# Chunk 0's block inverses: halves joined by small matmuls beside the first hops, and keys 7 and 8 loaded from GpSimd's queue

## The chip, the cores and the metric

The kernel runs on one core of a Trainium2 chip. The metric is device time in microseconds from launch to end. The core has five engines, each of which works through its own list of instructions in order: TensorE (PE: matrix products, which end in the accumulator memory PSUM), VectorE (DVE: elementwise work and reductions), ScalarE (ACT: functions and scaled copies), GpSimd (POOL: masks and a few elementwise operations) and SyncE (SP, which here only issues transfers). A transfer (DMA) is issued from the queue of an engine, here SP's or POOL's, and waits in that queue for what stands ahead of it. Engines wait for each other through semaphores.

## The reference, cut to what matters

Two parts. First a delta-rule attention over 4 batches, 8 heads, 768 positions and a head size of 48; then a feed-forward layer on its output (3072 tokens, 384 to 2048 to 384).

```python
k_n = k / (norm(k) + 1e-06)
for t in range(S):
    y[:, :, t] = einsum('bhd,bhde->bhe', q[:, :, t], state)
    v_old = einsum('bhde,bhd->bhe', state, k_n[:, :, t])
    state = state + beta[t] * einsum('bhd,bhe->bhde', k_n[:, :, t], v[:, :, t] - v_old)
h = x @ w_in
out = (h * sigmoid(1.702 * h)) @ w_out
```

The loop over positions is computed in chunks of 128. Within a chunk the recurrence is a lower triangular system per batch and head, with the scaled products of keys below its diagonal. The kernel cuts it into four blocks of 32 positions, inverts each 32x32 block on the diagonal, and applies the blocks one after another.

## The kernel before, in words

A unit is one chunk of one batch (all 8 heads); there are 24, numbered chunk by chunk, so units 0 to 3 are chunk 0 of batches 0 to 3. Per unit the key tile `KN` is turned into `kT` (`turn`, line 398), multiplied with itself into `G` (`gram`, line 375), and the queries `QP` are turned into `QS` and multiplied with the keys into the score matrix `M` (`scores`, line 565), which GpSimd masks (`select`, line 604).

`invert` (line 441) inverts all 128 diagonal blocks of a chunk at once, one (batch, head, block) in each partition, on DVE. `NT` holds the blocks, `YB` the growing inverses, each as 32x32 numbers in a row. First come 15 steps, each a product and a reduction, that invert the upper left and lower right 16x16 halves together. Then come eight pairs of a product and a reduction (`dots`, line 453) that work out the off-diagonal half from the two inverted halves and the 16x16 block between them. For chunk 0 the result is transposed by 32x32 squares (`YT`), so that partitions are positions again, and multiplied by the scale in `zs` into one tile `XB` for each unit.

The sequence of the blocks is done in hops. `together` (line 796) does, for one or two units, `solve` (block inverse times values, into `psU`, copied by ACT into `US`) and `below` (products that carry a solved block to those below it, into `psR`, subtracted from `V` by DVE). `hops(a, b)` (line 952) interleaves two units over eight hops. In chunk 0 units 0 and 1 go first, then units 2 and 3. After each pair `put_out` (line 960) computes outputs (`psY`), state (`ST`) and the transfers of the result into `xT`.

Beside this stands the conversion of the feed-forward weights. The weights arrive as 64-bit floats and are rebuilt as 32-bit ones on DVE and ACT, a step at each `fill` (line 294). `fetch_in` (line 174) fetches a quarter of `w_in` in twelve transfers; the fourth quarter is fetched when the first is converted (line 284), into the same place. `fetch_out` (line 190) does the same for `w_out`. `hidden` (line 700) and `written` (line 724) are the feed-forward products; `hidden` yields so that the products can be woven in (`feed`, line 1007).

The order of everything up to chunk 1 is written out by hand in the last part (from line 885), and most operations there are pinned to program order on their engine. `keys()` (line 965) normalizes and turns the keys of units 4 to 8 in small steps; `ahead_of(preparing, 1)` takes one. `warm` (line 132) issues matmuls with no use of their result: 46 of them (`NY`) in the middle of `invert`, then 11 (`NU`) in a hop of the first path, 3 (`NA`) in the last two. From unit 3 on `woven` (line 840) does the rest of the chunks.

Tiles come from pools with a fixed number of buffers. `spare` (line 437) takes a buffer of the pool `gT` (8 buffers) for other use in the start. `KN` has seven buffers, so key 7 goes where key 0 was, and 8 where 1 was. In the kernel before, keys 7 and 8 are loaded from SP after both outputs of the first pair.

## Time and profile before

| | |
|---|---|
| time, median of 3 runs | 781.71 us (781.21 to 783.49) |
| profiled execution, its own time | 782.82 us |
| its span, first to last instruction | 780.8 us |
| granted TensorE clock, mean | 0.965 |
| PE busy | 753.3 us (96%), 8165 matmul instructions |
| DVE busy | 457.1 us (59%) |
| ACT busy | 243.1 us (31%) |
| POOL busy | 125.3 us (16%) |
| shares of the chain that ended last | PE 83%, DVE 11%, DMA 3%, ACT 2%, issue 1% |
| first solve of chunk 0 (`psU`) starts at | 44.73 us |
| first output product of unit 0 (`psY`) starts at | 60.16 us |
| first output product of unit 2 starts at | 98.67 us |
| first DVE operation of chunk 1's inversion starts at | 114.95 us |

The profile gives the start of each instruction from the start of the span. A matmul of 32-bit floats is two instructions in it. Busy shares of a whole span say little here, because the start (up to some 160 us) is limited by other things than the rest. The chain of work that ended last is followed back from the end, at each step to what released the instruction; a filler matmul that nobody waits for can stand in it when it is the instruction before on PE. Nearly all instructions stand on one line (102, a helper that pins them), so they are told apart by the tiles that they write and read.

### The profile page before, as it was taken

To read this page: it belongs to the slowest core of one execution; us is meant where nothing else is said; L and a number is where in the kernel's file an instruction comes from. 1 tells how busy PE (TensorE), PEld (TensorE's weight loads), DVE (VectorE), ACT (ScalarE), POOL (GpSimd) and SP (SyncE) were. 2 spreads that over 40 slices of the span, in tenths; PEclk is the share of its full clock that TensorE was granted. 3 is DMA by queue.
4 is the path that set the end of the run, shared out by engine and by line. 5 is a ranking of instruction groups with operands and counts; after the bars stand their busy time and mean duration, and the time that the engine had idled before them with its cause. 6 is when DMAs were issued, how large, how long until landed. Compare 5 with 4: busy or idle time off the path is not lost.

```text
span 780.8 us, 18832 instructions
## 1 busy us (share of the span) xinstructions
PE 753.3 (96%) x8165; PEld 564.1 (72%) x8165; DVE 457.1 (59%) x935; ACT 243.1 (31%) x536; POOL 125.3 (16%) x130
## 2 busy tenths in 40 slices
PE   7898799699999999999999999999999999999997
PEld 6677688365678678678678678678678678687684
DVE  5989679987977566666666666666665531000000
ACT  4563642234333223123123123123123123121110
POOL 6311310011221221221221221221210000000000
PEclk8599899879999999999999999999999999999999
DMA  9954940453332142142142142142130020000000
GB/s 158 177 68 92 220 90 1 120 159 89 75 96 62 37 98 51 36 97 55 32 98 54 33 98 54 33 97 55 33 76 12 22 44 1 15 13 1 26 1 21
DMA packets 132610, 50.73 MB, mean 65 GB/s; under 512 B 107456, under 2 KB 128064, under 8 KB 132528
## 3 DMA queue, kind: packets, MB, share of 16 engines
q1 hardware_dynamic: 130192, 41.47, 25.1%
q0 software_dynamic: 2336, 8.06, 4.2%
q8 instruction: 64, 1.05, 0.6%
q14 instruction: 18, 0.15, 0.1%
HBM read 32.08 MB, written 16.25 MB: 62 GB/s over the span
## 4 chain that ended last, share of the span: by engine, by line
PE 83%; DVE 11%; DMA 3%; ACT 2%; issue 1%; SPq 0%; POOL 0%; DVEq 0%; POOLq 0%; ACTq 0%
PE po L102 29%; PE ph L102 27%; PE psU L102 5%; PE psY L102 5%; PE psQ L102 4%; PE psG L102 4%; PE psT L102 3%; DVE P L102 3%; PE ps_warm L102 2%; PE psR L102 2%; DVE YB L102 2%; DVE tmp L102 2%; DVE w_out L102 1%; DVE NT L102 1%; DMA KN<-in_k_dram 1%
## 5 line engine op out<-in xcount | busy, mean ns | idle before, releaser
L102 PE MATMUL po<-w_out,gT 128*128 128x384 f32 x768 | 269.6, 500 | 7.2 <-ACT ksq L102 5.2
L102 PE MATMUL ph<-xT,w_in 128*128 128x256 f32 x1152 | 262.6, 384 | 0.3
L102 PEld LDWEIGHTS ph<-xT,w_in 128*128 128x128 f32 x1152 | 215.6, 191 | 32.9 <-issue 1.3
L102 PEld LDWEIGHTS po<-w_out,gT 128*128 128x128 f32 x768 | 143.2, 193 | 99.3 <-ACT ksq L102 5.6
L102 DVE TENSOR_TENSOR V<-V,psR 64x384 f32<-64x384 f32 (+1 forms) x96 | 53.3, 556 | 193.2 <-PE psR L102 190.3
L102 ACT ACTIVATE gT<-ph 128x512 f32<-128x512 f32 x96 | 56.5, 596 | 140.1 <-PE ph L102 140.0
L102 DVE TENSOR_TENSOR P<-NT,YB 64x8 f32<-64x8 f32 (+31 forms) x190 | 89.5, 471 | 5.4
L102 ACT COPY US<-psU 32x384 f32<-32x384 f32 x92 | 43.2, 470 | 135.6 <-PE psR L102 123.8
L102 DVE TENSOR_REDUCE YB<-P 64x4 f32<-64x8 f32 (+31 forms) x190 | 80.9, 426 | 6.5
L102 PEld LDWEIGHTS psU<-V,XB 32*32 32x32 f32 x1536 | 58.1, 106 | 33.6 <-issue 28.9
L102 PE MATMUL psU<-V,XB 32*32 32x48 f32 x1536 | 68.7, 204 | 0.6 <-issue 0.3
L605 POOL TENSOR_SCALAR_AFFINE_SELECT M<-M 128x1024 f32<-128x1024 f32 x20 | 26.4, 1321 | 249.8 <-DVE M L102 170.3
L102 PE MATMUL psR<-US,G 32*32 32x48 f32 x2208 | 60.6, 204 | 0.0
L102 PEld LDWEIGHTS psR<-US,G 32*32 32x32 f32 x2208 | 51.2, 106 | 1.6 <-ACT w_out L102 1.1
L102 PE MATMUL psQ<-QS,kT 48*128 48x176 f32 (+1 forms) x384 | 37.6, 341 | 2.7 <-ACT QS L102 2.7
L102 PE MATMUL psG<-kT 48*128 48x128 f32 x384 | 33.6, 315 | 3.8 <-ACT kT L102 2.6
L102 PEld LDWEIGHTS psQ<-QS,kT 48*128 48x128 f32 x384 | 31.1, 209 | 5.9 <-ACT QS L102 4.4
L102 DVE TENSOR_TENSOR P<-NT 64x256 f32<-64x256 f32 (+7 forms) x40 | 34.5, 862 | 0.4
L102 PEld LDWEIGHTS psG<-kT 48*128 48x128 f32 x384 | 28.6, 214 | 7.7 <-ACT kT L102 3.0
L102 DVE TENSOR_REDUCE NT<-P 64x64 f32<-64x1024 f32 (+7 forms) x40 | 32.6, 815 | 1.4
L102 ACT COPY o<-po 128x384 f32<-128x384 f32 x24 | 11.5, 479 | 61.7 <-issue 39.2
L102 ACT COPY M<-psQ 128x256 f32<-128x256 f32 x68 | 22.9, 377 | 22.2 <-DVE V L102 16.1
(98 smaller groups left out, 602.8 us busy)
## 6 DMA issues: line engine op xcount, KB each, us to landing
Nd<-G SPq DMA_DIRECT2D x16, 512.0 KB, 3.5
QP<-in_q_dram SPq DMA_DIRECT2D x24, 192.0 KB, 4.2
V<-in_v_dram SPq DMA_DIRECT2D x24, 192.0 KB, 3.4
out_dram<-o SPq DMA_DIRECT2D x24, 192.0 KB, 2.5
NT<-Nd SPq DMA_DIRECT2D x20, 128.0 KB, 2.6
Yd<-YS SPq DMA_DIRECT2D x20, 128.0 KB, 2.5
XB<-Yd SPq DMA_DIRECT2D x20, 128.0 KB, 3.0
KN<-in_k_dram POOLq DMA_DIRECT2D x13, 192.0 KB, 3.7
```

The costliest lines, as they stand in the source:

```text
L102: return lambda *a, **kw: tc.keep_in_program_order(op(*a, **kw))
L605: (pool if self.n < B else nc.gpsimd).affine_select(out=self.M, in_=self.M, compare_op=ALU.is_gt, fill=0.0, base=0, pattern=[[0, H], [1, 1 ...
```

## The change

For chunk 0, `invert` ends after the 15 steps on the halves. DVE then transposes the inverted halves twice: `YT` with positions of the block's rows in the partitions, and `Yb`, the same blocks the other way round. The off-diagonal half of each unit is made by the new function `joined`: for each head and block a 32x32 by 32x16 product on PE with the diagonal block in `D_`, an ACT copy back into `D_`, a second product with `Yb` (16 rows contracted), a subtraction on DVE into `YT`, and the product with the scale that gives `XB`. A unit's join is 64 matmuls, in two stages of 32.

The joins of unit 0 and the first stage of unit 1 stand ahead of the first hop; the others go into the hops of the first path. So do the scores of unit 1 and the first part of those of unit 2, and the scaling of the values of units 2 and 3; the rest of the scores of units 2 and 3 goes into the second path. Fillers in `invert` become 30, issued after the DVE steps in program order; in hops 0 to 5 of the first path they become 5.

The order of the first transfers changes: values 0 and 1 and query 0 go before the first quarter of `w_in`, GpSimd waits for value 1 (`landed`) before the second quarter, keys 4 to 6 go ahead of the third quarter. Keys 7 and 8 are loaded by GpSimd's queue, each after the output of the unit whose buffer it takes. `zs` moves from the pool slot `ksq` into the buffer that `late_U` uses, and the small ACT operation at the start uses the gelu function instead of a copy.

```diff
--- before.py
+++ after.py
@@ -55,7 +55,7 @@
     GB = 8
 
     XR = DP - D
-    NW, NA, NY, NU = 14, 3, 46, 11
+    NW, NA, NY, NU = 14, 3, 30, 11
     NQ = DFF // 4
     NPC = DFF // 8
     NS = C * C + C
@@ -137,7 +137,7 @@
             pe.matmul(ps, lhsT=ones[:, 0:128], rhs=ones, start=True, stop=True)
 
     table = cpool.tile([128, 1], F32, name="table")
-    act.activation(table, ident[:, 0:1], ACT.Copy)
+    act.activation(table, ident[:, 0:1], ACT.Gelu_apprx_sigmoid)
 
     w_out = cpool.tile([128, FC, DM], F32, name="w_out")
 
@@ -477,6 +477,11 @@
             red(diag(Yf, i, [[BS, i]]), P, axis=AX.X, op=ALU.add, negate=True)
             yield 0.0
 
+        if c == 0:
+            vec.transpose(YT.rearrange("p d i -> p i d"), Y.rearrange("p j i -> p i j"))
+            vec.transpose(Yb.rearrange("p d j -> p j d"), Y)
+            yield 0.0
+            return
 
         X1 = N[:, 0:HS, HS:]
         if c <= 1:
@@ -497,8 +502,6 @@
             yield 0.0
         for i in range(0, HS, Q):
             n = i + Q
-            if c == 0 and i == HS - 3 * Q:
-                warm(NY, vec.memset)
             dots(
                 Y[:, 0:HS, HS + i : HS + i + Q],
                 A[:, :, 0:n].rearrange("p j (o l) -> p j o l", o=1).broadcast_to([np, HS, Q, n]),
@@ -506,18 +509,6 @@
                 HS, Q, n, True,
             )
             yield 0.0
-        if c == 0:
-            T = wk.tile([128, BS, BS], F32, tag="P", name="YT")
-            vec.transpose(T.rearrange("p d i -> p i d"), Y.rearrange("p j i -> p i j"))
-            for b in range(B):
-                XB = wk.tile([128, H, BS], F32, tag="XB", name="XB", bufs=4)
-                tt(
-                    XB, T[:, b * H : (b + 1) * H],
-                    zs[:, 5, b].broadcast_to([128, H, BS]), op=ALU.mult,
-                )
-                inverse[b] = XB
-                yield 0.0
-            return
         YS = wk.tile([128, BS, BS], F32, tag="P", name="YS")[part]
         tt(YS, Y, bc, op=ALU.mult)
         dma = sync if c < 3 else nc.sync.dma_start
@@ -536,6 +527,35 @@
                 inverse[c * B + b] = XB
         yield 0.0
 
+
+    def joined(b):
+
+        HS = BS // 2
+        d = slice(b * H, (b + 1) * H)
+        blocks = [slice(blk * BS, (blk + 1) * BS) for blk in range(NB)]
+        ps = ps_moe.tile([128, H, HS], F32, tag="moe", name="psZ")
+        for h in range(H):
+            for r in blocks:
+                pe.matmul(
+                    ps[r, h, :], lhsT=D_[r, b, h, :], rhs=YT[r, b * H + h, HS:],
+                    start=True, stop=True,
+                )
+        Z = D_[:, b, :, 0:HS]
+        act.copy(Z, ps)
+        yield
+        ps = ps_moe.tile([128, H, HS], F32, tag="moe", name="psC")
+        for h in range(H):
+            for r in blocks:
+                u = slice(r.start, r.start + HS)
+                pe.matmul(
+                    ps[r, h, :], lhsT=Yb[u, b * H + h, :], rhs=Z[u, h, :],
+                    start=True, stop=True,
+                )
+        vec.tensor_tensor(YT[:, d, HS:], YT[:, d, HS:], ps, op=ALU.subtract)
+        XB = wk.tile([128, H, BS], F32, tag="XB", name="XB", bufs=4)
+        vec.tensor_tensor(XB, YT[:, d], zs[:, 5, b].broadcast_to([128, H, BS]), op=ALU.mult)
+        inverse[b] = XB
+        yield
 
     def bank(name, shape=(128, H, D)):
         return ps_seq.tile(list(shape), F32, tag="seq", name=name)
@@ -904,21 +924,31 @@
         pool.memset(KN[i][:, :, D:DP], 0.0)
     landed = cpool.tile([128, 1], F32, name="landed")
     pool.tensor_copy(landed, KN[B - 1][:, 0, 0:1])
+    def first_queries(b):
+        load(b, ((QP, q),), sync)
+
+    for b in range(HB):
+        load_values(b, sync)
+    first_queries(0)
     fetch_in(0, other_queue)
-    for b in range(B):
-        load(b, ((QP, q),), sync)
-    for b in range(B):
+    pool.tensor_copy(landed, loaded[HB - 1][:, 0, 0:1])
+    for b in range(1, B):
+        first_queries(b)
+    for b in range(HB, B):
         load_values(b, sync)
     fetch_in(1, other_queue)
-    D_ = spare("blocks").rearrange("p (b h k) -> p b h k", b=B, k=BS)
-    fetch_in(2, other_queue)
     for n in range(B, len(KN)):
         load(n, ((KN, k),), sync)
+    D_ = spare("blocks").rearrange("p (b h k) -> p b h k", b=B, k=BS)
+    YT = spare("YT").rearrange("p (d i) -> p d i", i=BS)
+    Yb = spare("Yb").rearrange("p (d i) -> p d i", i=BS)
+    fetch_in(2, other_queue)
     for blk in range(NB):
         sync(out=bI[blk::NB, 1:], in_=betas[:, 1:, blk, :])
-    late_U = spare("U")[:, 0 : H * D + XR]
+    room = spare("U")
+    late_U = room[:, 0 : H * D + XR]
     pool.memset(late_U[:, H * D :], 0.0)
-    zs = wk.tile([128, 6, B, H], F32, tag="ksq", name="zs", bufs=1)
+    zs = room[:, 512 : 512 + 6 * B * H].rearrange("p (s b h) -> p s b h", s=6, b=B)
     psD = [ps_seq.tile([128, B, NP, BS], F32, tag="seq", name="psD") for _ in range(2)]
     warm(NW)
     for b in range(B):
@@ -935,19 +965,26 @@
     vec.transpose(
         NT.rearrange("p i k -> p k i"), D_.rearrange("p b h k -> p k (b h)")
     )
-    for b in range(B):
+    def values_scaled(s, hs):
+        for h in hs:
+            act.mul(s.V[:, h, :], s.V[:, h, :], zs[:, 4, s.b, h : h + 1])
+
+    for b in range(HB):
         gram(b)
-    inverting = invert(0)
-    pair = [new_step(n) for n in range(B)]
-    for n in range(B):
-        for _ in pair[n].scored:
-            pass
-    run(inverting)
-    for s in pair:
-        for h in range(H):
-            act.mul(s.V[:, h, :], s.V[:, h, :], zs[:, 4, s.b, h : h + 1])
-    for s in pair:
-        s.select()
+    pair = [new_step(n) for n in range(HB)]
+    run(pair[0].scored)
+    pair[0].select()
+    for b in range(HB, B):
+        gram(b)
+    pair += [new_step(n) for n in range(HB, B)]
+    for s in pair[:HB]:
+        values_scaled(s, range(H))
+    run(invert(0))
+    warm(NY)
+    joins = [joined(b) for b in range(B)]
+    next(joins[0])
+    next(joins[1])
+    next(joins[0])
 
     def hops(a, b):
 
@@ -986,17 +1023,29 @@
 
     preparing = keys()
     path = hops(*pair[:2])
+    beside_hops = {
+        0: lambda: next(joins[1]),
+        1: lambda: next(pair[1].scored),
+        2: lambda: (run(pair[1].scored), pair[1].select()),
+        3: lambda: next(joins[2]),
+        4: lambda: next(joins[3]),
+        5: lambda: next(joins[2]),
+        6: lambda: next(joins[3]),
+        7: lambda: next(pair[2].scored),
+    }
     for i in range(2 * NB):
         together(*next(path))
+        beside_hops[i]()
         fill(1)
         if i > 1:
             ahead_of(preparing, 1)
-        warm(NU if i < 6 else NA)
-    for s in pair[:2]:
+        if 3 <= i < 7:
+            values_scaled(pair[2 + (i - 3) // 2], range((i - 3) % 2 * NP, (i - 3) % 2 * NP + NP))
+        warm(NU // 2 if i < 6 else NA)
+    for n, s in enumerate(pair[:2]):
         put_out(s)
+        load(len(KN) + n, ((KN, k),), other_queue)
         fill(2)
-    load(7, ((KN, k),), sync)
-    load(8, ((KN, k),), sync)
     for n in range(B, B + 2):
         load(n, ((QP, q),), sync)
     for n in range(B, B + 2):
@@ -1017,8 +1066,14 @@
     gTs = [], []
     ffn.append(hidden(xTs[0], gTs[0], slice(0, NTH), 1.3, True))
     path = hops(*pair[2:])
+    beside_hops = {
+        0: lambda: (run(pair[2].scored), pair[2].select()),
+        1: lambda: next(pair[3].scored),
+        2: lambda: (run(pair[3].scored), pair[3].select()),
+    }
     for i in range(2 * NB):
         together(*next(path))
+        beside_hops.pop(i, lambda: None)()
         fill(2 if i < 5 else 3)
         if i > 2:
             feed()
```

## The prediction

> **What bounds the kernel now.** I read the page's slices first: the first seven show PE below full, its granted clock falling to half, and DVE near full. Then the chain that ended last, DVE's timeline for the stretch the chain shows as filler matmuls, and the busy time by stretch.

> The page's slices (one digit is a tenth of busy share, 19.5 us a slice):

> ```profile
> PE   7898799699999999999999999999999999999997
> DVE  5989679987977566666666666666665531000000
> PEclk8599899879999999999999999999999999999999
> ```

> DVE's timeline (start, length, then the instruction): the second half of chunk 0's inversion.

> ```profile
> 27.67 0.77 DVE L102 COPY NT<-YB 128x256 f32<-128x256 f32 x1
> ...
> 40.92 1.22 DVE L102 TENSOR_REDUCE YB<-P 128x64 f32<-128x1024 f32 x1
> 42.17 1.99 DVE L102 STREAM_TRANSPOSE YT<-YB 128x1024 f32<-128x1024 f32 x1
> 44.20 1.43 DVE L102 TENSOR_TENSOR XB<-YT,zs 128x256 f32<-128x256 f32 x4
> ```

> The chain over the same time and a later one:

> ```profile
> 37.77 6.60 PE ps_warm L102 x46
> 44.38 0.35 issue
> 44.73 0.83 PE psU L102 x16
> 45.56 1.31 PE ps_warm L102 x11
> 47.68 1.31 PE ps_warm L102 x11
> ...
> 70.91 4.03 DMA w_out<-in_moe_w_in_dram
> 75.00 5.62 DMA KN<-in_k_dram
> 80.70 0.52 ACT ksq L102
> 81.25 0.61 ACT G L102
> 81.90 1.12 PE psT L102 x4
> ```

> The chain names fillers, but they end at 44.38 and wait for nobody; the first solve at 44.73 needs XB, which DVE begins only at 44.20. So DVE's inversion, 16.76 to 44.6, sets the start of the hops. The second block is a transfer: key loads stand on SP behind twelve fetches of w_in, and ACT, in order, waits for one (7.2 us in the waits).

> Busy time by stretch (DVE's is the third figure):

> ```profile
> 30.00:40.00 10.00, 8.63 (x53) 6.64 (x52) 9.76 (x15) 5.98 (x20) 4.03 (x3) 0.50 1.03 187
> 60.00:70.00 10.00, 8.66 (x189) 7.66 (x186) 9.74 (x18) 5.28 (x13) 1.64 (x1) 1.00 0.05 13
> 70.00:80.00 10.00, 7.94 (x153) 6.00 (x151) 7.72 (x13) 2.15 (x4) 1.64 (x1) 0.83 1.09 197
> 80.00:90.00 10.00, 8.10 (x107) 6.46 (x108) 3.93 (x9) 7.12 (x12) 6.41 (x8) 0.66 1.18 252
> ```

> After the clock column come DMA share and GB/s: DMA is idle at 60 to 70, saturated at 70 to 90 while ACT waits, PE runs at 0.66 and DVE at 39%. From psY of unit 2 (98.67) on, DVE works almost without a gap to 162 and PE without one to 139; a shift there goes to the end.

> [...] the 46 fillers took 6.6 us; at 0.226 us (14 cold ones took 3.17) and 0.119 us (11 warm ones took 1.31) some 10 were cold. Short waits (1.34 and 0.68 us from 67.7 on) were enough to halve it at 71.5. [...] psD agrees, 64 instructions in 0.82 us, but with four column groups and one row group. [...] a key load takes a median 3.7 us from GpSimd, 4.6 from SP.

> **The change, part by part.**

> *Before the first hop.* DVE stops after its triangular steps (27.63), transposes YT (1.99, to 29.7) and Yb (the same shape, to 31.7). 14.5 us of DVE products go away. PE keeps four grams but only unit 0's score ahead of the fillers: the second gram ends at 16.87 as now, the score takes 3.8 (the period of the four at 22.5 to 37.7), two grams 2.83 each, so fillers begin at 26.4 and 30 of them (10 cold, 20 warm) take 4.7: 31.2. ACT scales 16 value slices, not 32 (7.32/2 = 3.7), done by about 31. Then the join of unit 0: a stage of 32 matmuls is 64 instructions. By psD's rate 64 x 12.8 ns = 0.82 us. The first stage of unit 0 to 32.0, of unit 1 to 32.8 with unit 0's ACT copy beside it (128x128, as `last`, 0.27), the second stage of unit 0 to 33.7, DVE's subtraction 0.3 (nearest: ST 128x192, 0.36), the XB product 1.43/4 = 0.36, handovers 0.1 each: the first solve at about 34.8 instead of 44.73. **-9.9.** Bounds: 33.3 if PE is early (DVE's transposes then rule); 40 if a stage costs 52 ns an instruction, as psU in one tile (16 in 0.83).

> This needs V0, V1 and Q0 early. They go on SP right after keys and beta (6.24), ahead of the first fetch, so 0.6 MB at the 137 GB/s of that stretch take 4.3 us; I take about 14, PE asks at 17. GpSimd now waits for V1 before its second fetch; behind it stand fetches and unit 0's mask, needed only at its output.

> *The first eight hops.* PE fills each now: 0.83 + 1.31 = 2.12; first solve to psY is 44.73 to 60.16 = 15.4. New fillers are five (0.6), and the rest goes in: hop 0 takes the second stage of unit 1, and hop 1 waits for its XB (0.83 + 0.82 + 0.3 + 0.4 + handovers = 2.5); hop 1 transposes (0.83 + 0.66 + 0.6 = 2.1, also DVE's two 0.57 subtractions); hop 2 has psQ (0.83 + 1.44 + 0.6 = 2.9); hops 3 to 5 a stage each (2.25; ACT has about 2.6 in hop 3 with copy, Relu 0.94, four scalings 0.9, so 0.2 over), hop 6 with three fillers 2.0, hop 7 1.9. Sum 18.2. **+2.8.** Keys 4 to 6 are issued ahead of the third fetch instead of after it; at today's place (issued 40.35, landing some 4.6 later) ACT would stop for them in hop 2, at about 40.

> *Outputs and second hops 0 to 2.* Today 60.16 to 76.25 = 16.1, with DVE full from 58.3 to 72, PE waiting, then at half clock. The PE work alone: outputs 2.8; hops 0.83 x 3 + fillers 1.31 x 3 + psT 0.66 x 2 + psG 1.16 x 2 = 10; added scores of units 2 and 3, 1.44 x 2 + 0.66 = 3.5, total 15. DVE's demand from first solve to here is 23 plus 3 x 0.7, against PE's 33: DVE no longer rules. **-1.** So hop 3 begins at about 68, not 76.25.

> *Keys 7 and 8.* Their buffers are keys 0 and 1, free after each state product (61.7 and 63.0 now, some 54 and 56 after). GpSimd issues them there, before the w_in fetches, instead of at 75; behind each stand unit 2's mask and the `rn` powers, which wait no longer than that product. Landing 3.7 to 5.6 later, 58 to 62, before hop 2 asks at about 65. Hops 3 to 7 took 76.25 to 98.67 = 22.4; their PE work at full clock is 3.1 + 3.5 + 2.7 + 4.7 + 2.3 = 16.3. **-6.1.** SP's Q and V loads behind the two keys move up by 2 us.

> *The table load.* 1.28 us of ACT at 85 goes to the start, where a load stands anyway. Copy, Square and Relu run after it without another load, so one set holds all. PE's idle covers it: 0; at most -1.3.

> Sum: -9.9 + 2.8 - 1 - 6.1 = -14.2. I give back 2.4 for PE to ACT round trips, which such sums leave out (4.6 us of psT waiting for G at 60 to 120 now, of which the keys explain 3.3, plus ACT's extra copies). **-11.8.** The profiled execution took 782.82 (span 780.8 and 2.0 outside), so 771.0. The median of the runs is 781.71, 1.1 less: **770**.

> **Rivals.**

> *Only the start gains.* ACT becomes the bound of the hops, with 3.2 us more copies in the second path, or key 8 lands amid the w_in fetches and still stops it. For: 252 GB/s at 80 to 90, Q landings of 12 to 17 us early on. Against: DMA is idle at 50 to 65. The 6.1 and some of the rest are lost: 777.

> *The joins run one tile after another, and it gets slower.* Each matmul of a stage lies in another row and column group and all write one bank; no row here shows that pattern. At psU's 52 ns a stage takes 3.3, not 0.82: eight stages, 20 us, all on PE's path: about 790. It decides above 0.82 + 11.8/8 = 2.3 us a stage. Against: in hop 1, solves and products in four column groups run at 13.6 ns an instruction (64 in 0.87).

> *The clock stays half.* Five fillers for eleven, with waits for ACT and DVE. At half clock a hop of 2.2 costs about 1.8 more; five cold hops eat 9: 779. For: the fall at 71.5. Against: each hop has 1.4 to 2.9 us of PE work and waits under 0.9.

> *The start gains nothing.* V1 or Q0 land after 20 and PE's queue stands there; each microsecond past 17 costs one. With 10 late: 781, the change without effect.

> **How the numbers follow.** The forecast's case (766 to 775): 0.60. Only the start or half the gain (775 to 779.3): 0.19. Still better, 760 to 766, if round trips hide: 0.07. No change: 0.05. Slower by serial joins, or by clock and late loads: 0.09. A measurement here can't tell less than 0.3%, 2.3 us. Faster 0.86, same 0.05, slower 0.09. The range 763 to 779.5 holds the first case, nearly all of the second and a little of the third, 0.8.

> **What would show it.** First solve at 34 to 36; join stages under 1 us each; first solve to psY about 18; ACT's wait for keys gone or under 2; granted clock 1.0 at 35 to 80; no table load at 85; psY of unit 2 near 86; the inversion of chunk 1 starting near 103 instead of 115. Wrong if a join stage takes 2 us or more, if the clock reads 0.5 within the hops, if ACT waits for a key again, or if the chain shows V or QP loads before 35.

## The result, and the profile after

| | before | after |
|---|---|---|
| time, median of 20 runs of each, taken side by side | 783.2 us | 784.71 us |
| ratio, with its 95% interval | | 1.0017 [0.9993, 1.0041] |
| profiled execution, its span | 780.8 us | 782.9 us |
| granted TensorE clock, mean | 0.965 | 0.964 |
| first solve of chunk 0 (`psU`) | 44.73 us | 34.66 us |
| first output product of unit 0 (`psY`) | 60.16 us | 66.27 us |
| first output product of unit 2 | 98.67 us | 100.83 us |
| from there to the end of the span | 682.1 us | 682.1 us |

The change makes no difference that can be measured, where 770 us was forecast. The last row says where to look: the whole difference of the two traces, 2.1 us, is made before unit 2's outputs, and the rest of the kernel runs as before. The first solve comes 10.1 us sooner, the first eight hops take 31.6 us instead of 15.4, and the second path (unit 0's `psY` to unit 2's) takes 34.6 instead of 38.5. The first and the last of these three steps came out near their forecast size. The middle one ate everything.

The slices of the page after (a digit is a tenth of busy share, 19.6 us a slice):

```profile
PE   7889999688999999999999999999999999999997
DVE  6747889996977666666666666666655531000000
PEclk8657999999999999999999999999999999999999
```

Before, the third and fourth slices (39 to 78 us) had PE at 9 and 8 with a clock of 9 in both. Now PE is at 8 and 9 with a clock of 5 and 7: it is busy because it is slow.

The start, in the timeline after (start, length, engine, instruction; in brackets the idle time ahead of it and what ended it):

```profile
28.83 1.97 DVE L102 STREAM_TRANSPOSE YT<-YB 128x1024 f32<-128x1024 f32 x1
...
31.93 1.29 PE L102 MATMUL psZ<-YT,blocks 32*32 32x16 f32 x128
33.09 0.72 PE L102 MATMUL psC<-blocks,Yb 16*32 16x16 f32 x64
34.18 0.43 DVE L102 TENSOR_TENSOR XB<-YT,U 128x256 f32<-128x256 f32 x1
34.66 0.65 PE L102 MATMUL psU<-V,XB 32*32 32x48 f32 x11 [0.86 <-DVE XB L102]
```

This answers to the DVE lines of before, where the transpose stood at 42.17 and `XB` at 44.20. Two first stages (128 instructions) take 1.29 us and a second stage (64) 0.72, 10 and 11 ns an instruction where `psU` in one tile took 52 before. So the tiles do overlap, and the join costs what the sum said.

Then the chain that ended last, over hops 0 and 1:

```profile
34.66 0.65 PE psU L102 x11
35.31 1.66 issue
...
40.65 2.08 issue
43.24 1.05 PE psT L102 x4
44.29 1.07 PE ps_warm L102 x5
```

Twice, for 1.66 and 2.08 us, PE stands in the middle of a group of matmuls and waits for nothing that the profile shows ("issue"). Four `psT` products take 1.05 us, where they took 0.66 at full clock. The stretches say how long that lasts (busy time of PE, of its weight loads, DVE, ACT, POOL, then granted clock, DMA share, GB/s):

```profile
40.00:50.00 10.00, 7.92 (x139) 6.03 (x132) 4.12 (x6) 4.08 (x9) 0.46 (x1) 0.50 0.51 102
50.00:60.00 10.00, 10.00 (x335) 8.27 (x335) 4.63 (x9) 5.91 (x19) 2.31 (x2) 0.50 0.02 5
60.00:70.00 10.00, 10.00 (x191) 8.62 (x190) 6.19 (x12) 3.55 (x11) 2.60 (x2) 0.60 0.01 2
```

From 50 to 66 us PE's record has no gap, hardly a transfer runs beside it (DMA share 0.01 to 0.02), DVE and ACT are half idle, and the clock stays at 0.50. Set beside the forecast hop by hop (a hop ends with its fillers; the ends are read from the chain):

| hop | beside the solves | forecast, us | measured, us | difference, and what stands in it |
|---|---|---|---|---|
| 0 | second stage of unit 1 | 2.5 | 4.7 | +2.2: the 1.66 wait |
| 1 | `psT` of unit 1 | 2.1 | 6.0 | +3.9: the 2.08 wait, half clock |
| 2 | `psQ` of unit 1 | 2.9 | 4.6 | +1.7: half clock |
| 3, 4, 5 | one join stage each | 2.25 each | 3.4 each | +3.5: half clock |
| 6, 7 | join stage; `psT` of unit 2 | 3.9 | 6.1 | +2.2: half clock |
| sum | | 18.2 | 31.6 | +13.4 |

So there are two suspects: a clock that falls at about 37 us and does not come back before the path ends (it is whole again from 67.9), and waits in which PE may lack instructions. From here on these are called waits for instructions; what speaks for that stands further down. The runs take the two apart.

### The profile page after: what moved, and what is told of

Its sections match the earlier page's. It is cut to its first block, busy times and chain, and to the rows that moved or that the text cites. A ratio compares the mean times of both kernels' runs of the same rounds, so it can differ in the third digit from the quotient of the medians.

```text
span 782.9 us, 19754 instructions
## 1 busy us (share of the span) xinstructions
PE 752.8 (96%) x8625; PEld 564.8 (72%) x8625; DVE 449.1 (57%) x922; ACT 242.0 (31%) x539; POOL 127.0 (16%) x133
## 4 chain that ended last, share of the span: by engine, by line
PE 83%; DVE 12%; issue 2%; ACT 1%; DMA 0%; POOL 0%; DVEq 0%; POOLq 0%; ACTq 0%; SPq 0%
PE po L102 29%; PE ph L102 27%; PE psU L102 6%; PE psY L102 5%; PE psQ L102 4%; PE psG L102 4%; PE psT L102 3%; DVE P L102 3%; PE ps_warm L102 2%; DVE w_out L102 2%; DVE YB L102 2%; PE psR L102 2%; DVE tmp L102 2%; DVE NT L102 1%; DVE V L102 1%
## 5 line engine op out<-in xcount | busy, mean ns | idle before, releaser
L102 PE MATMUL po<-w_out,gT 128*128 128x384 f32 x768 | 267.4, 497 | 9.6 <-ACT ksq L102 5.1
L102 PE MATMUL ph<-xT,w_in 128*128 128x256 f32 x1152 | 261.2, 383 | 0.3
L102 PEld LDWEIGHTS ph<-xT,w_in 128*128 128x128 f32 x1152 | 214.9, 190 | 32.5 <-issue 1.7
L102 PEld LDWEIGHTS po<-w_out,gT 128*128 128x128 f32 x768 | 142.0, 192 | 101.5 <-DVE w_out L102 7.8
L102 DVE TENSOR_TENSOR V<-V,psR 64x384 f32<-64x384 f32 (+1 forms) x96 | 53.3, 556 | 199.2 <-PE psR L102 198.0
L102 ACT ACTIVATE gT<-ph 128x512 f32<-128x512 f32 x96 | 56.4, 595 | 138.9 <-PE ph L102 138.8
L102 DVE TENSOR_TENSOR P<-NT,YB 64x18 f32<-64x18 f32 (+25 forms) x186 | 86.3, 464 | 5.4
L102 PEld LDWEIGHTS psU<-V,XB 32*32 32x32 f32 x1536 | 61.0, 109 | 36.8 <-issue 29.6
L102 ACT COPY US<-psU 32x384 f32<-32x384 f32 x92 | 43.2, 469 | 142.4 <-PE psR L102 124.0
L102 DVE TENSOR_REDUCE YB<-P 64x6 f32<-64x18 f32 (+25 forms) x186 | 77.7, 418 | 6.4
L102 PE MATMUL psU<-V,XB 32*32 32x48 f32 x1536 | 72.3, 208 | 2.6 <-issue 1.7
L102 PE MATMUL psR<-US,G 32*32 32x48 f32 x2208 | 64.0, 209 | 2.1 <-issue 2.1
L102 PEld LDWEIGHTS psR<-US,G 32*32 32x32 f32 x2208 | 54.3, 110 | 3.4 <-issue 2.8
L102 PE MATMUL psQ<-QS,kT 48*128 48x176 f32 (+1 forms) x384 | 36.2, 329 | 1.3 <-ACT QS L102 0.9
L102 PE MATMUL psG<-kT 48*128 48x128 f32 x384 | 32.5, 308 | 3.8 <-ACT kT L102 1.7
L102 PEld LDWEIGHTS psG<-kT 48*128 48x128 f32 x384 | 27.5, 208 | 7.3 <-ACT kT L102 2.1
L102 PEld LDWEIGHTS psQ<-QS,kT 48*128 48x128 f32 x384 | 29.7, 198 | 3.7 <-ACT QS L102 1.5
L102 ACT COPY o<-po 128x384 f32<-128x384 f32 x24 | 11.5, 478 | 61.8 <-issue 39.2
L102 DVE TENSOR_TENSOR P<-NT 64x256 f32<-64x256 f32 (+7 forms) x36 | 30.3, 842 | 0.4
L102 DVE TENSOR_REDUCE NT<-P 64x64 f32<-64x1024 f32 (+7 forms) x36 | 29.3, 814 | 1.2
L87 POOL DMA_DIRECT2D KN<-in_k_dram x13 | 12.4, 953 | 104.9 <-PE psY L102 96.0
```

The costliest lines, as they stand in the source:

```text
L87: dma(out=dst[n % len(dst)][:, :, 0:D], in_=src[b, :, c * C : (c + 1) * C, :].rearrange("h p d -> p h d"),)
L102: return lambda *a, **kw: tc.keep_in_program_order(op(*a, **kw))
```

## The experiments

In every run four times are read from the trace: the first solve, the length of the path (first solve to unit 0's `psY`), unit 2's `psY`, and PE's waits that end with "issue" in the path. Each ratio is to the kernel before, run on the same chip.

**Eleven fillers again in hops 0 to 5** (`after_f11`). If the clock is the cause, six more fillers per hop should shorten the path, though they are work.

```diff
-        warm(NU // 2 if i < 6 else NA)
+        warm(NU if i < 6 else NA)
```

> The changed kernel with eleven fillers instead of five in hops 0 to 5. Theory 'fillers' (the clock, once lost near 37 us, can't come back on five fillers a hop): the granted clock is back at 1.0 by about 45 to 50, first solve to first psY takes 22 to 26 us instead of 31.7, unit 2's psY comes near 94 to 97 instead of 100.9, and the whole is 4 to 8 us faster than the changed kernel, 0.990 to 0.996 of before. Theory 'hop work' (the hops are long because more work stands in each, at any clock): six more fillers add 0.7 us to each of six hops, 4 us slower than the changed kernel, about 1.007 of before.

Measured: 779.42 us, ratio 0.9948 [0.9921, 0.9974]. First solve at 33.70, path 26.8, unit 2's `psY` at 93.81. More work made the path 4.8 us shorter, though it stayed longer than the 22 to 26 us that were expected. Its stretches, in the same columns:

```profile
40.00:45.00 5.00, 4.65 (x97) 3.61 (x99) 2.06 (x3) 1.12 (x3) 0.00 (x0) 0.62 0.90 175
45.00:50.00 5.00, 5.00 (x153) 4.22 (x156) 3.31 (x5) 3.24 (x9) 1.40 (x1) 1.00 0.33 64
```

The clock is whole from 45 us on, and the hops with a join stage there take 2.7 to 3.3 us, close to the 2.25 of the forecast and six fillers of 0.119. But 26.8 is far from 15.4, and PE waits four times for instructions: 1.07, 1.08, 0.38 and 0.75 us. The clock is one cause, and not the only one.

**Five fillers in the kernel before** (`before_f5`): do five fillers fail by themselves, with no joins?

```diff
-        warm(NU if i < 6 else NA)
+        warm(NU // 2 if i < 6 else NA)
```

> The kernel before with five fillers instead of eleven in hops 0 to 5 of its first path, nothing else. Theory 'fillers': its clock, whole at 44.7, falls to 0.5 within the path even without a wait on PE, the path takes 18 us or more instead of 15.4, total 1 to 5 us more than before. Theory 'idle waits' (only PE's waits of 1.7 and 2.1 us took the clock away, and five fillers would hold a clock that is whole): clock stays 1.0, the path takes 13 to 14.5 us, total the same as before or up to 2 us less, since DVE sets the time after it.

Measured: 784.71 us, ratio 1.0020 [0.9998, 1.0042]; path 18.0 instead of 15.4. With 36 fillers less it ought to have been 4.3 shorter, had nothing else changed. Its stretches:

```profile
50.00:55.00 5.00, 4.74 (x111) 3.44 (x111) 3.84 (x6) 2.83 (x5) 0.00 (x0) 0.67 0.03 7
55.00:60.00 5.00, 5.00 (x75) 3.56 (x73) 3.31 (x6) 1.40 (x4) 1.68 (x1) 0.50 0.00 0
```

The fall comes after a wait for instructions of 1.29 us ahead of it, and afterwards the record shows PE busy for all 5.00 us while the clock is 0.50. Solves and five fillers did not restore the clock before 65 us (0.50 from 60 to 65), after the path. That they would not hold it without the wait is not shown here: the expectation named a fall "even without a wait on PE", and there was one. With eleven fillers a longer wait did no harm: in `f11_sp78` (below) PE waits 1.86 us at 49.3, and the clock is 1.00 all the way from 43 to 60. The prediction's "against" for this rival, that each hop has 1.4 to 2.9 us of PE work, was no argument: the record can be as busy as it was from 55 to 60 us here, all 5.00 us, with the clock at 0.50.

**Keys 7 and 8 alone** (`before_k78`): the kernel before with only this part of the change.

```diff
-    for s in pair[:2]:
+    for n, s in enumerate(pair[:2]):
         put_out(s)
+        load(len(KN) + n, ((KN, k),), other_queue)
         fill(2)
-    load(7, ((KN, k),), sync)
-    load(8, ((KN, k),), sync)
```

> The kernel before with only keys 7 and 8 moved to GpSimd's queue, each after the output of the unit whose buffer it takes. Theory 'keys' (that wait was worth what the prediction gave it): ACT's 7.2 us wait for a key at 80 goes, psY of unit 2 comes at 92 to 95 instead of 98.67, total 0.992 to 0.996 of before. Rival: the fetches of w_in or DVE take the place of the wait, psY of unit 2 at 97 or later, total within 0.2%.

Measured: 777.22 us, ratio 0.9924 [0.9895, 0.9953]. The first path is untouched (15.43), GpSimd issues the keys at 63.40, and unit 2's `psY` stands at 91.73 instead of 98.67. The stretches from 75 to 85 us of this kernel:

```profile
75.00:80.00 5.00, 5.00 (x125) 4.33 (x124) 4.12 (x9) 3.54 (x7) 0.75 (x1) 1.00 0.92 175
80.00:85.00 5.00, 5.00 (x75) 4.06 (x75) 4.77 (x11) 4.02 (x7) 4.98 (x7) 1.00 0.98 245
```

and of the kernel before:

```profile
75.00:80.00 5.00, 3.62 (x73) 2.77 (x70) 3.82 (x8) 0.00 (x0) 0.00 (x0) 1.00 1.20 178
80.00:85.00 5.00, 3.10 (x54) 2.57 (x55) 1.03 (x2) 4.17 (x8) 3.11 (x4) 0.67 1.43 184
```

In the kernel before, ACT did nothing for 5 us, and PE stood idle for 3.3 of the 10; with the keys early PE has no gap and the clock stays whole. Unit 2's outputs come 6.9 us earlier, where the prediction had put 6.1 on this part, and a little ahead of the expected 92 to 95. That is more than the whole change brings, and it needs no joins.

**The keys back on SP, joins and eleven fillers kept** (`f11_sp78`): what the rest of the change brings when the clock is held.

```diff
 (after_f11)
-        load(len(KN) + n, ((KN, k),), other_queue)
         fill(2)
+    load(7, ((KN, k),), sync)
+    load(8, ((KN, k),), sync)
```

> The changed kernel with eleven fillers and with keys 7 and 8 back on SP, after both outputs, as in the kernel before. Theory 'the two parts add': the wait of ACT for a key is back, 4 to 8 us, psY of unit 2 at 98 to 101, total 0.999 to 1.006 of before, that is, the joins by themselves bring nothing even with a whole clock. Rival: in the changed kernel the keys don't matter, since PE sets its second path; total within 0.2% of the run with eleven fillers and keys on GpSimd's queue.

Measured: 782.69 us, ratio 0.9979 [0.9960, 0.9998]; path 27.7, unit 2's `psY` at 97.58, ACT waits 3.5 us for a key. The keys are worth 97.58 - 93.81 = 3.8 us here. What is left, the joins with eleven fillers, the new order at the start and the table load, gains 1.1 us at unit 2's `psY`: 11.2 at the first solve and 2.1 in the second path, of which the first path takes 12.2 back. In the total that is 0.2%. Neither expectation was met: the wait is a little shorter than 4 us and the whole a little faster than 0.999, yet the keys do matter.

**The third fetch later** (`after_late`), **and the second and third later, with five fillers** (`late2`), **with eleven** (`f11_late2`), **and with unit 1's score also moved ahead of the first solve** (`f11_late2_s1`). These asked whether the waits for instructions come from the weight transfers that run at the same time.

```diff
 (after_late)
-    fetch_in(2, other_queue)
+    quarter(2)
 (hop loop)
+        if i == 3: fetch_in(2, other_queue)
 (late2, f11_late2 and f11_late2_s1: in place of the line with i == 3)
-    fetch_in(1, other_queue)
+        if i in (2, 4): fetch_in(i // 2, other_queue)
 (f11_late2_s1: also, ahead of the third gram; NY = 16, nothing beside hops 1 and 2)
+    run(pair[1].scored)
+    pair[1].select()
```

> The changed kernel, five fillers, with the third quarter of w_in fetched in hop 3 instead of before the first hop, so that few transfers run at 35 to 43 us. Theory 'transfers hold up PE's instructions': PE's two waits without a releaser (1.7 us at 35.3, 2.1 at 40.7) shrink below 0.5 each, the path is at least 3 us shorter; whether the clock then holds tells if the waits took it away. Rival: the waits stay, for they belong to the new runs of small matmuls; path 30 to 32 us, total within 0.3% of the changed kernel.

> The changed kernel, five fillers, with the second and third quarter of w_in fetched in hops 2 and 4, so that by 34 us all earlier transfers should have landed. Theory 'transfers hold up PE's instructions': no PE wait without a releaser above 0.8 us between the first solve and hop 2. Theory 'fillers': the clock falls to 0.5 within the path all the same, as five fillers and small matmuls don't hold it, and the path takes 24 us or more. Theory 'waits took the clock': with the waits gone the clock stays whole, path 18 to 20 us, total 0.985 to 0.990 of before.

> The same fetches in hops 2 and 4, and eleven fillers. If the waits for instructions come from the load of transfers and the fillers hold the clock, both losses are gone: clock 1.0 from the first solve on, path 22 to 23.5 us (26.8 with eleven fillers alone), psY of unit 2 at 88 to 91, total 0.987 to 0.991 of before. Rival: runs of small matmuls wait for instructions at any load, path 25 us or more, total about 0.995 as with the fillers alone.

> As the run with both late fetches and eleven fillers, and the score of unit 1 taken out of hops 1 and 2 and put before the fillers ahead of the joins, with 16 fillers there instead of 30. The path loses 0.66 and 1.44 us of PE: 2 to 3 us shorter than with the score in the hops, the first solve within 1 us of 34 if the query of unit 1 has landed by 22; total 0.984 to 0.989 of before. Rival: PE waits for that query or ACT's copies are late, first solve at 36 or later, and the two cancel.

| | ratio | first solve, us | path, us | PE's waits for instructions, us |
|---|---|---|---|---|
| `after_late` | 1.0042 [1.0019, 1.0064] | 34.55 | 31.9 | 3.27, 0.24 |
| `late2` | 1.0048 [1.0021, 1.0075] | 34.23 | 32.4 | 1.78, 1.43, 0.49, 0.30 |
| `f11_late2` | 1.0038 [1.0022, 1.0054] | 34.57 | 34.3 | 3.90, 2.02, 1.06 |
| `f11_late2_s1` | 1.0035 [1.0021, 1.0049] | 35.73 | 34.1 | 5.69, 0.78, 0.74 |

All four are slower than the kernel before. None saw the first wait go, and the path lengths fit the rivals in `after_late` (30 to 32 us) and `f11_late2` (25 or more). But none tests what it was made for. Half of each fetch is issued by SP, and SP's half waits for nothing on PE: in `f11_late2` SP issued it from 30.98 to 33.87, ahead of the first solve at 34.57, as SP's timeline there shows.

```profile
30.98 2.89 SPq L102 DMA_DIRECT2D raw<-in_moe_w_in_dram  x6
```

Only GpSimd's half came later, so transfers still filled the DMA through the first wait: until about 38 us in `after_late` and `f11_late2`, 40 in `late2` and 45 in `f11_late2_s1` (its DMA share is 1.02 to 1.08 from 32 to 44). Why the first wait is longer in these runs than in `after` is taken up with the packets below.

**Small matmuls in the kernel before, and as much PE time in fillers** (`before_mm`, `before_w18`; one execution each). Both add about the same PE time to each hop: one as 32 small unread matmuls between solves and fillers, the other as seven more fillers. They part the number of instructions from the time.

```diff
 (before_mm: in each hop, ahead of the fillers)
+        small()   # for h in range(H): for blk in range(NB):
+                  #   pe.matmul(ps[r, h, :], lhsT=ident[r, 0:BS], rhs=ident[r, 0:16])
 (before_w18)
-        warm(NU if i < 6 else NA)
+        warm(NU + 7 if i < 6 else NA + 7)
```

> The kernel before, with a stage of 32 matmuls of 32x32 by 32x16 that nobody reads put into each of the eight hops of the first path (128 instructions, 0.82 us a hop by the rate of psD), fillers as before. Theory 'blocks of instructions' (PE's instructions come in blocks of 256, and a hop that needs more than about one block in 3.7 us waits for the next): PE waits without a releaser inside the path, each 256 recorded PE instructions after the last possible one, and the path takes 25 us or more. Theory 'PE time only': 15.4 + 8 x 0.82 = 22 us, no such wait.

> The kernel before with seven more fillers in each hop of the first path: the same 0.83 us of PE a hop as 32 small matmuls, but 14 instructions instead of 128. Both theories: 15.4 + 8 x 0.83 = 22 us, no wait of PE without a releaser, clock 1.0. If this path is also 25 us or more, it isn't the number of instructions.

Measured: path 27.2 us with the small matmuls, 21.2 with the fillers, and 15.4 without either. With the fillers PE never waits for instructions in the path. With the small matmuls it does so six times, 4.6 us in all, though no transfer of note runs (DMA share 0.01 from 55 to 60). The other 1.4 us of the 6.0 between the two go with the clock, which reads 0.5 from 46.9 to 50.3 in `before_mm`, after a wait of 1.93 us for ACT ahead of the first solve, and again from 70.7 on. Two of the six in PE's timeline of `before_mm`:

```profile
57.10 0.20 PE L102 MATMUL psU<-V,XB 32*32 32x48 f32 x1 [1.18 <-issue]
60.83 0.20 PE L102 MATMUL psU<-V,XB 32*32 32x48 f32 x1 [0.79 <-issue]
```

The two are 3.7 us apart. Counting PE's records (matmuls, weight loads and its semaphore instructions together) from the start of the trace up to each such wait, in this kernel and in the other fourteen (`before` has one of 1.96 us, at 9.80), gives only these counts:

```
449  1217  1473  1729  1985  2241  2497  2753      all 193 more than a multiple of 256
```

```profile
q8 instruction: 64, 1.05, 0.6%
```

and after:

```profile
q8 instruction: 68, 1.11, 0.6%
```

(packets, MB, share). A packet is 16.4 KB. PE's matmuls and weight loads are 2 x 8165 before and 2 x 8625 after, 255 and 254 to a packet, and at 256 to a packet the change's 920 further ones make just under four more. The waits in the paths stand where PE has many records in a short time: a hop of before, with no such wait, has at most 150 records in 2.1 us, a hop with a join stage up to 247 in 2.7 us (`after_f11`), a hop of `before_mm` up to 278 in 3.1. With an idle DMA the boundary waits of `before_mm` are 0.2 to 1.2 us, one about every 3.5 to 4 us. Under the transfers of the first hops they are 0.8 to 5.7.

The traces also hold each packet of q8 with its time. While PE runs through one block of `before_mm` (57.11 to 60.83), the only transfer of the core is one such packet, which starts at 58.25 and takes 1.15 us:

```profile
q8 instruction: 1, 0.02, 1.9%
```

So here the packet starts only 1.1 us after PE has entered the block, and PE enters the next one 1.4 us after the packet's end. In all 30 boundary waits of the paths the packet takes 0.9 to 1.8 us, and PE goes on 1.3 to 1.8 us after its end. What differs is how long after PE's entry the packet starts: 0.6 to 1.6 us in the 11 waits where hardly anything else was transferred meanwhile (DMA share 0.00), 0.9 to 5.5 in the 19 where the DMA share was 0.76 or more. In `after_late`, `f11_late2` and `f11_late2_s1` the packet ahead of the first wait starts 3.6, 3.7 and 5.5 us after PE's entry, with a DMA share of 1.0 to 1.2. That the transfers lengthen the waits by holding up this packet is what the packets suggest; no run isolates it, since the four late runs did not take the transfers away.

**Four matmuls a stage instead of 32** (`few`, five fillers; `f11_few`, eleven; one execution each). Both leave part of the join out: one product per block for all eight heads, with head 0's block for all of them, so the joined halves of seven heads are not the reference's. The order of the steps and the waits between them stay as they were.

```diff
-        for h in range(H):
-            for r in blocks:
-                pe.matmul(ps[r, h, :], lhsT=D_[r, b, h, :], rhs=YT[r, b * H + h, HS:], ...)
+        for r in blocks:
+            pe.matmul(ps[r], lhsT=D_[r, b, 0, :], rhs=YT[r, d, HS:], ...)
 (and so the second stage; f11_few: NU fillers)
```

> The changed kernel, five fillers, with four matmuls in each join stage instead of 32 (one head's weights applied to all heads, so the joined halves are those of head 0 and the output is not the reference's): 16 instructions a stage instead of 128, everything else as it was. Theory 'blocks of instructions': the waits at the first hops go or move later, since 450 instructions less stand before hop 2; path shorter by 4 us or more. On the clock: if it still falls to 0.5 with no wait above 1 us in the path, five fillers can't hold it by themselves; if it stays 1.0, the waits took it away, path about 16 to 19 us.

> The changed kernel with four matmuls in a join stage instead of 32 (head 0's weights for all heads, so the joined halves are not the reference's) and eleven fillers: the fourth corner of fillers and small matmuls. If the clock and the blocks of instructions together are all that the prediction's sum of the hops left out, the sum holds here: 18.2 + 6 x 0.71 for the fillers - 5 x 0.6 for the stages in the path = 19.5 us, within 1 us, with the clock at 1.0 throughout and no wait of PE for instructions. If the path is 21.5 or more, the hops wait for ACT or DVE beyond that sum, and a third cause is open.

| path, us (PE's waits for instructions) | 32 matmuls a stage | 4 matmuls a stage |
|---|---|---|
| 5 fillers | 31.6 (1.66, 2.08) | 24.6 (none) |
| 11 fillers | 26.8 (1.07, 1.08, 0.38, 0.75) | 21.5 (none) |

With four matmuls a stage, PE no longer waits for instructions, and the clock is still lost with five fillers (`few`):

```profile
50.00:55.00 5.00, 5.00 (x76) 3.16 (x71) 3.41 (x8) 3.25 (x11) 1.42 (x1) 0.50 0.00 0
```

With eleven it comes back (`f11_few`):

```profile
40.00:45.00 5.00, 5.00 (x120) 3.96 (x121) 2.06 (x3) 2.09 (x6) 0.73 (x1) 0.79 1.24 178
45.00:50.00 5.00, 5.00 (x163) 3.98 (x155) 3.23 (x5) 3.76 (x12) 0.68 (x1) 1.00 0.50 79
```

So both causes are there, and each acts without the other. Fewer instructions save 7.0 and 5.3 us (3.7 and 3.3 of it are the waits, the rest PE's own time for the stages), more fillers 4.8 and 3.1, after the 36 x 0.119 = 4.3 us that they take themselves. With both mended, the prediction's own terms come to 19.5 us for the path, and 21.5 was measured. That is just where the expectation had put a third cause, and it had asked for a whole clock, which was at 0.5 from 35.3 to 42.1. The hops show that this is where the 2.0 us lie: hop 1, wholly at half clock, takes 4.8 us instead of 2.8, and every other hop is within 0.2 us of its terms. PE's record from 35 on in `f11_few` leaves no room for a wait for ACT or DVE. `f11_few` took 773.76 us, with 780.2 for the kernel before beside it. Unit 2's `psY` stands at 88.36 there, 3.2 us ahead of the same with keys and table load alone (91.56, next run): that is what the joins might have brought, had a stage cost 4 matmuls instead of 32.

**Keys and table load, no joins** (`k78_gelu`): the parts of the change without its core.

```diff
 (before_k78)
-    act.activation(table, ident[:, 0:1], ACT.Copy)
+    act.activation(table, ident[:, 0:1], ACT.Gelu_apprx_sigmoid)
```

> The kernel before with keys 7 and 8 on GpSimd's queue and the table loaded at the start by the gelu function, no joins. Theory 'hidden': the load of 1.28 us on ACT in the second path stands beside PE's work, total as with the keys alone, 0.9924, within 0.2%. Rival: ACT is on the path there, up to 1.3 us less, 0.991. Either way faster than both kernels.

Measured: 776.37 us, ratio 0.9901 [0.9872, 0.9929]. This is the fastest complete version of the study, ahead of both kernels. It cannot be told from the keys alone (0.9924 [0.9895, 0.9953]), so the expectation "hidden" and its rival are not told apart; unit 2's `psY` stands at 91.56 and 91.73 in the two.

## Why the prediction was wrong

**The start, -9.9.** Right: -10.1. Stages of 0.65 to 0.72 us instead of 0.82, the first solve at 34.66 in the announced 34 to 36. The rival "one tile after another" (3.3 us a stage) is refuted, and so is "the start gains nothing": no load of `V` or `QP` is late. (The bound of 40 us for slow stages counts two of them; three stand on PE ahead of the first solve, which gives 42. It did not come into play.)

**The first eight hops, 18.2 us or +2.8.** This is the step that failed: 31.6 us, +16.2. It added up PE work at the rates of the kernel before and took for granted that PE would have its clock and its instructions. Neither holds. The clock: the prediction named the sign ("if the clock reads 0.5 within the hops"), had seen it at half after waits of 1.34 and 0.68 us, and had a rival for it, with five cold hops and 9 us. It was seven hops at half clock and part of the first, and what the removed fillers had done for the clock was put at nothing: only their time was counted. The instructions: a stage was priced as 64 x 12.8 ns, and no term or rival asked how the 128 further PE records of a stage (64 matmul instructions and their weight loads) are supplied. The rate of 12.8 ns was read from `psD`, and even there the kernel before had its one wait at a block boundary (9.80, 1.96 us), which the prediction passed over. Of the 13.4 us beyond the forecast, 3.7 are the two waits for instructions. The other 9.7 lie where PE's record has no such wait, nearly all of it with the clock at 0.50, and 7.4 of them in hops 2 to 7, where it has no wait at all. `f11_few`, which takes the waits away and brings the clock back, comes within 2.0 us of the prediction's terms, so the sum itself was sound. What took the clock away at 37 us is open: it falls at 35.5 and 35.3 in `few` and `f11_few` too, where PE does not wait for instructions.

**Outputs and second path, -1 - 6.1 and 2.4 given back, in all -4.7.** The sum is near, -3.9, but not part by part. From unit 0's `psY` to hop 3 of the second path it takes 18.7 us (66.27 to 84.97) where it took 16.1, so +2.6 instead of -1. The prediction's terms there add up to 16.3 (2.8 + 10 + 3.5) and not to the 15 that it wrote, so even they gave +0.2. Hops 3 to 7 take 15.9, so -6.6 instead of -6.1. With the keys alone they take the same 15.9, after an unchanged 16.1, so this gain is the keys'. The stretch that grew is the one into which the scores were moved, and the clock is still at 0.5 in its first 1.6 us; how much each costs was not separated. The 2.4 us given back for other reasons cover most of this miss, and that is luck. ACT's 7.2 us wait for a key is gone. The rival "only the start gains" had it the wrong way round: the keys' gain came, and the first path used up that of the start.

**The table load, 0.** Right. It is gone from 85 us, and `k78_gelu` shows no difference that can be told from none.

**A shift at unit 2's `psY` goes to the end.** Right: 2.2 us there, 2.1 us of span.

The sum as measured is -10.1 + 16.2 - 3.9 = +2.2. The range (763 to 779.5) did not hold it. The rival that came nearest, "the clock stays half" (779), had one of the two causes, at 9 of the 13.4 us that the step was short; with the 3.7 us of instruction waits beside it, it would have gone beyond the range.

## What to carry to other kernels

Moving work from an engine that is full to PE counts instructions as well as time. In these runs PE waited at block boundaries that came 256 records and 3.2 to 4.0 us apart with an idle DMA, and 3.8 to 8.4 us apart under transfers; a stretch that would issue its records faster than that is to be checked for such waits. Few wide products in place of many small ones took the waits away and the path from 31.6 to 24.6 us with five fillers, from 26.8 to 21.5 with eleven, though with joins that were not the reference's. Fillers that nobody waits for are not free to cut: with five the clock read 0.50 from 37.2 us to the end of the path, with eleven it was whole again from 45 us, so change their number alone first and read the granted clock. And take a change apart before it is judged as a whole: here two moved loads brought 0.8% by themselves, and with the rest beside them nothing was left.

## What had not been expected of the hardware

PE's record can be full while its clock is halved. From 50 to 65 us of `after` the record has no gap, and the clock is 0.50 for the 15 us. A full record did not bring the clock back in these hops: with five fillers PE is busy without a gap from 43 to 67 us in `after` and from 35.6 to 59 in `few`, and the clock reads 0.50 all that time. With eleven it is back 6.8 us after its fall, or sooner, in `after_f11`, `f11_sp78` and `f11_few`, but not always: in `f11_late2_s1`, also with eleven, PE is busy for 11.7 of the 11.8 us from 48.0 to 59.8, with no wait for instructions after 48.1, and the clock reads 0.50 throughout. So the number of fillers matters (`after` against `after_f11`, `few` against `f11_few`), and what brings the clock back stays open. The profile models the ends of matmuls, so a row of short products may look fuller in it than it is; whether that plays a part was not shown. Nor did the fall take a wait above 0.86 us: in `few` it comes at 35.5 after waits of 0.59, 0.86 and 0.24 us.

The waits at block boundaries, from 0.2 to 5.69 us, are the second.

A third had no effect here. One product of DVE's inversion takes 1.86 us in `after`

```profile
23.88 1.86 DVE L102 TENSOR_TENSOR P<-NT,YB 128x338 f32<-128x338 f32 x1
```

and 0.51 us before:

```profile
24.06 0.51 DVE L102 TENSOR_TENSOR P<-NT,YB 128x338 f32<-128x338 f32 x1
```

In `after` GpSimd's mask of unit 0 (24.25 to 25.36) lies in that time, in the kernel before it does not. DVE's transposes therefore start at 28.83 instead of the 27.6 of the forecast, but PE's own work ahead of the joins ends only at 32.0, so nobody waited for them. (In `few` and `f11_few`, whose stages on PE are shorter, PE waits 0.59 and 0.88 us for `Yb`.) That GpSimd's operation is the cause was not tested. Other traces agree: in `f11_few` the mask lies over a 128x450 product, which takes 1.63 us instead of 0.63, and in `before` a mask that starts 0.17 us after a 128x768 product takes 1.73 us instead of 1.09, while the product keeps its 0.95.
